# Decode attention for two blocks of 32 heads on one core: the output projection with `wo` as the moving operand

## The chip, the core and the metric

The program runs on one core of one Trainium2 chip. The metric is device time in microseconds (us) of one execution, and lower is better. Before the change the median of three timed runs is 668.55 us (668.42 to 668.57).

## What is computed

Two independent attention blocks, A and B, decode one token each and their outputs are laid side by side. Cut to what matters, for each block:

```python
q = (x @ wq).reshape(1, 1, 32, 128).transpose(0, 2, 1, 3)          # x: 1x512, wq: 512x4096
scores = einsum("bhqd,bhkd->bhqk", q, k_cache) * 128 ** -0.5       # k_cache: 32 heads x 8192 x 128
o = einsum("bhqk,bhkd->bhqd", softmax(scores), v_cache)            # v_cache: 32 heads x 8192 x 128
y = o.transpose(0, 2, 1, 3).reshape(1, 1, 32 * 128) @ wo           # wo: 4096x512
out = concatenate([y_A, y_B], axis=-1)                             # 1 x 1 x 1024
```

Everything is bfloat16. The caches of the two blocks hold 268 MB of the 285 MB that are read.

## The kernel before, in words

The 64 heads are handled in `NM` = 16 *quads* of `G` = 4 heads, 8 quads of A and then 8 of B. Quad n's keys lie in `kn[:, n % 2]` and its values in `vn`. In both, a partition holds 256 consecutive tokens of one head, and 32 partitions hold a head.

For each quad VectorE multiplies the keys by the query in four pieces (`plan_mul`, L333), and TensorE folds each product with 16 matmuls against the identity (`plan_red`, L342). VectorE sums what is left (`plan_sr`, L353), the maximum goes round all engines (L359, L365, L368, L378, L382), and ScalarE takes the exponentials (L390). TensorE then sums the exponentials over partitions (`plan_sum`, L395) and multiplies them with the values in 256 matmuls whose stationary operand is a block of V and whose moving operand is 4 columns wide (`plan_pv`, L411). `plan_o` (L421) scales the result into `oD`, where a head is a column and its 128 elements are the partitions. PV of quad n-1 stands within quad n's folding, so PV of quad 15 comes last, after the loop.

`wo`, cut into groups of heads by `WOG`, is loaded behind the last keys into the key buffer that has come free: A as one group of 32 heads, B as groups 0 to 6 with 8, 4, 4, 8, 4, 2 and 2 heads. The loads lie on SyncE's one queue in this order: keys of quad 15, `wo` of A, B's groups 0 and 1, the last values in three parts (128, 64 and 64 of the 256 blocks of PV), B's groups 2 to 6. The last values are issued when PV of quad 14 has ended.

The `wo` load puts the 4096 input rows of a group on partitions in another order than `oD` has them, so a *relayout* (`plan_relayout`) turns a group's outputs into `o2`: VectorE spreads the columns over `zb` with a mask (L446), TensorE multiplies `zb` with a selection matrix `jsel` into `misc` (L450), and VectorE copies `misc` to `o2` (L452). `zb` has two slots, `misc` one. Relayouts stand one after the other.

`plan_wo` (L463) then makes, for every head j and every quarter i of the 512 outputs, one matmul: the 128x128 block of `wo` is stationary, the column `o2[:, a, j]` moves, and the four sums stand in `qyp[:, 0:4]` with the outputs on partitions. `plan_y` (L470) copies them to `yT`. `plan_out` turns `yT` of both blocks with one matmul against the identity (L474), copies the 8x128 result to `out_q` (L477) and writes it out.

The order of this end is written out by hand. Between the last maximum and the last PV stand: the relayouts of A and of B's groups 0 and 1, `plan_wo` of A (128 matmuls), `plan_y(0)`, `plan_wo` of B's groups 0 and 1 (48 matmuls), and the relayouts of B's groups 2, 3 and 4. This piece is called *the early piece* below. After the last PV and `plan_o` stand `plan_wo` of B's groups 2, 3, 4 (64 matmuls), the relayouts and `plan_wo` of groups 5 and 6 (16 matmuls), `plan_y(1)` and `plan_out`. This is called *the tail*. TensorE's program is a loop over quads. It leaves the loop for the early piece (the `Else` branch at L593), comes back into the loop body for the last PV, and leaves it again for the tail.

Of the kernel before, what the change touches and what calls it, by code (L numbers as in the profile page):

```python
# [6 lines left out]
ALU = mybir.AluOpType  # L7
AX = mybir.AxisListType
BF16 = mybir.dt.bfloat16
F32 = mybir.dt.float32  # L10

P = 128
# [11 lines left out]
class _Plan:  # L24
# [6 lines left out]
    def wait(self, eng, mark):  # L31
        if mark is None:
            return
        ctr, val = mark
        if val <= 0 or self.waited.get((eng, ctr.name), 0) >= val:
            return
        self.waited[(eng, ctr.name)] = val
        self.prog[eng].append((None, ctr, val))

    def op(self, eng, fn, ctr=None, needs=(), inc=1):  # L40

        for m in needs:
            self.wait(eng, m)
        self.prog[eng].append((fn, ctr, inc))
        if ctr is None:
            return None
        ctr.n += inc
        return ctr, ctr.n
# [81 lines left out]
def bass_concat_heads__mha_block_cached__gqa_block_cached__decode_kernel(  # L130
# [18 lines left out]
    NA = 2  # L149
    H, Sk, Dh = ks[0].shape[1:]  # L150
# [6 lines left out]
    G = 4  # L157
# [3 lines left out]
    QA = H // G  # L161
    NM = NA * QA
    NK = 2
    CT = 64
    NCH = T // CT
# [3 lines left out]
    WOG = [[(0, 32)], [(0, 8), (8, 4), (12, 4), (16, 8), (24, 4), (28, 2), (30, 2)]]  # L169
    BEFORE = 2  # L170
# [3 lines left out]
    with ExitStack() as st:  # L174
# [3 lines left out]
        def sb(name, shape, dt):  # L178
            return ec(nc.sbuf_tensor(name, shape, dt))

        kn = sb("kn", [P, NK, T, Dh], BF16)
        vn = sb("vn", [P, T, Dh], BF16)

        def flat(ap):
            return ap.rearrange("p t d -> p (t d)")
# [6 lines left out]
        wo_sb = [flat(kn[:, KW])[:, a * W:(a + 1) * W].rearrange("p (j n) -> p j n", n=NOUT)  # L192
                 for a in range(NA)]
# [7 lines left out]
        ident = sb("ident", [P, P], BF16)  # L201
# [6 lines left out]
        rinv = sb("rinv", [P, NM, G], F32)  # L208
        oD = sb("oD", [P, NA, H], BF16)
        zb = sb("zb", [P, 2, P], BF16)  # L210
        o2 = sb("o2", [P, NA, H], BF16)
        mask = {g: sb("mask%d" % g, [P, P // g], BF16) for g in RG}
        jsel = {g: sb("jsel%d" % g, [P, g], BF16) for g in RG}
        NQ = NOUT // P
        yT = sb("yT", [P, NA, NQ], BF16)
        out_q = sb("out_q", [NA * NQ, P], BF16)

        def ps(name, shape):
            return ec(nc.psum_tensor(name, shape, F32))
# [3 lines left out]
        mtp = ps("mtp", [P, 512])  # L223
        bmp = ps("bmp", [P, 512])
        misc = ps("misc", [P, 512])
        qyp = ps("qyp", [P, 512])

        pl = _Plan()
        op, wait = pl.op, pl.wait

        def ctr(name):
            return _Ctr(nc, st, name)
# [6 lines left out]
        s_out = ctr("s_out")  # L239
        c_pool, c_dve, c_act, c_pe = ctr("c_pool"), ctr("c_dve"), ctr("c_act"), ctr("c_pe")  # L240
        c_mul, c_red, c_sr, c_pv = ctr("c_mul"), ctr("c_red"), ctr("c_sr"), ctr("c_pv")

        def dma(eng, dst, src, c, needs=()):
            return op(eng, lambda e: e.dma_start(dst, src), c, needs, inc=16)  # L244


        def const(fn, needs=()):
# [5 lines left out]
            out=ident[:], in_=ones_bf[:], pattern=[[1, P]], compare_op=ALU.is_equal,  # L253
            fill=0.0, base=0, channel_multiplier=-1), [i_onesb])
        i_identf = const(lambda e: e.affine_select(
            out=ident_f[:], in_=ones_f[:], pattern=[[1, P]], compare_op=ALU.is_equal,
# [10 lines left out]
        red_done, pv_done, q_done, wo_done = {}, {}, {}, {}  # L267
# [18 lines left out]
        def load_wo(a, g):  # L286
            h0, n = WOG[a][g]
            src = wos[a][h0 * Dh:(h0 + n) * Dh, :].rearrange("(p j) n -> p (j n)", p=P)
            wo_in[a, g] = dma("SP", wo_sb[a][:, h0:h0 + n, :].rearrange("p j n -> p (j n)"), src,
                              s_wo[a][g], [red_done[NM - 2, NCH - 1]])  # L290


        for a in range(NA):
# [6 lines left out]
            m = op("PE", xmm, c_pe, [x_in, i_onesb])  # L300
            x_ready = op("ACT", lambda e, a=a: e.copy(
                xb[:, a].rearrange("p c m -> p (c m)"), (misc if a == 0 else qyp)[:]), c_act, [m])
        misc_free, qy_free = [x_ready], [x_ready]
# [25 lines left out]
        mul_done, sr_done, p_done, m_done, r_done, o_done = {}, {}, {}, {}, {}, {}  # L329
# [32 lines left out]
        gm_done = {}  # L362
# [9 lines left out]
        nb_done = {}  # L372
# [46 lines left out]
        def plan_o(n):  # L419
            a, i = divmod(n, QA)  # L420
            o_done[n] = op("DVE", lambda e: e.tensor_tensor(  # L421
                oD[:, a, G * i:G * (i + 1)], acc[:, 0:G], rinv[:, n, :], ALU.mult),
                c_dve, [pv_done[n], r_done[n]])


        sel_ready = {}
# [7 lines left out]
                    jsel[g][:], v.rearrange("p s j -> p j s"), AX.X, ALU.max), c_dve)  # L434

        z_n = [0]
        z_free = {}
        o2_ready = {}

        def plan_relayout(a, g):  # L440
            h0, n = WOG[a][g]
            z = z_n[0] % 2
            z_n[0] += 1
            s = P // n
            zv = zb[:, z, :].rearrange("p (h s) -> p h s", s=s)
            m = op("DVE", lambda e: e.tensor_tensor(  # L446
                zv, oD[:, a, h0:h0 + n].unsqueeze(2).broadcast_to([P, n, s]),
                mask[n][:, None, :].broadcast_to([P, n, s]), ALU.mult),
                c_dve, [sel_ready[n], o_done[a * QA + (h0 + n) // G - 1 if (h0 + n) % G == 0 else a * QA + (h0 + n) // G], z_free.get(z)])
            z_free[z] = op("PE", lambda e: e.matmul(misc[:, 0:n], zb[:, z, :], jsel[n][:],  # L450
                                                    start=True, stop=True), c_pe, [m, misc_free[0]])
            o2_ready[a, g] = misc_free[0] = op("DVE", lambda e: e.tensor_copy(  # L452
                o2[:, a, h0:h0 + n], misc[:, 0:n]), c_dve, [z_free[z]])

        def plan_wo(a, g):

            h0, n = WOG[a][g]

            def mm(e):
                r = None  # L460
                for j in range(h0, h0 + n):
                    for i in range(NQ):
                        r = e.matmul(qyp[:, i:i + 1], wo_sb[a][:, j, i * P:(i + 1) * P],  # L463
                                     o2[:, a, j:j + 1], start=(j == 0 and i == 0),
                                     stop=(j == H - 1 and i == NQ - 1), skip_group_check=True)
                return r
            wo_done[a] = op("PE", mm, c_pe, [o2_ready[a, g], wo_in[a, g], qy_free[0]])

        def plan_y(a):
            qy_free[0] = op("DVE", lambda e: e.tensor_copy(yT[:, a, :], qyp[:, 0:NQ]), c_dve,  # L470
                            [wo_done[a]])

        def plan_out():
            m = op("PE", lambda e: e.matmul(bmp[0:NA * NQ, 0:P], yT[:].rearrange("p a q -> p (a q)"),  # L474
                                            ident[:], start=True, stop=True),
                   c_pe, [qy_free[0], nb_done[NM - 1]])
            m = op("DVE", lambda e: e.tensor_copy(out_q[:], bmp[0:NA * NQ, 0:P]), c_dve, [m])  # L477
            done = dma("SP", out[0].rearrange("o (q n) -> (o q) n", q=NA * NQ), out_q[:], s_out, [m])
            wait("SP", done)


# [45 lines left out]
        NB = len(WOG[1])  # L527
        early = [g for g, (h0, n) in enumerate(WOG[1]) if h0 + n <= H - G]
        for g in range(BEFORE, NB):
            load_wo(1, g)  # L530
        plan_relayout(0, 0)
        for g in range(BEFORE):
            plan_relayout(1, g)
        plan_wo(0, 0)
        plan_y(0)
        for g in range(BEFORE):
            plan_wo(1, g)
        for g in early[BEFORE:]:
            plan_relayout(1, g)
        wait("PE", misc_free[0])  # L540
        cuts[NM].append(len(pl.prog["PE"]))
        plan_sum(NM - 1)
# [1 line left out]
            plan_pv(NM - 1, t0, t1)  # L544
        cuts[NM].append(len(pl.prog["PE"]))
        plan_o(NM - 1)
        for g in early[BEFORE:]:
            plan_wo(1, g)
        for g in range(len(early), NB):
            plan_relayout(1, g)  # L550
        for g in range(len(early), NB):
            plan_wo(1, g)
        plan_y(1)
        plan_out()

        for name, at in (("SP", block.sync), ("PE", block.tensor), ("ACT", block.scalar),
# [66 lines left out]
```

## Time and profile before

| what | value |
|---|---|
| median of three timed runs | 668.55 us |
| the profiled execution's own time | 668.41 us |
| its span, first to last instruction | 666.7 us |
| data read, mean rate over the span | 285.21 MB, 428 GB/s |
| TensorE, VectorE, ScalarE busy | 66 %, 51 %, 9 % |
| mean granted TensorE clock | 0.775 |
| chain that ended last, by engine | DMA 62 %, PE 25 %, DVE 10 % |

Times in the profile are in us from the start of the span. PE is TensorE's matmul, PEld its load of the stationary operand, DVE is VectorE, ACT ScalarE, POOL GpSimd, SPq SyncE's queue. `L463` is line 463 of the kernel before. A group's row has its busy time, the mean duration of one instruction in ns, and the idle time of its engine just before it. In a shape such as `128*128 128x512` the first pair is the stationary operand (partitions * columns) and the second the moving operand or the output (partitions x columns). The granted clock is a share of TensorE's full clock.

### The profile page before, as it was taken

The page shows a single profiled execution, that of the slowest core. Times are in us where ns is not written, and L with a number is a line of the kernel's source. Part 1 is how long each engine was busy: PE and PEld are TensorE (multiplying, and loading weights), DVE is VectorE, ACT ScalarE, POOL GpSimd, SP SyncE. Part 2 cuts the span into 40 slices and gives each one's busy share as a digit, 9 for nine tenths or more (in the row PEclk, how much of TensorE's full clock was granted, in tenths as well). Part 3 has the DMA queues.
Part 4 walks back from the last instruction along what each step waited for, and adds up shares of the span by engine and source line. Part 5 has one row for each costly group of instructions (what it writes and reads, how often), then busy time and mean ns, then how long its engine had stood idle before and what let it go on. Part 6 is the DMA issues. An engine that isn't in the chain of part 4 may idle for free.

```text
span 666.7 us, 12274 instructions
## 1 busy us (share of the span) xinstructions
PE 441.5 (66%) x5649; PEld 252.7 (38%) x5649; DVE 341.5 (51%) x221; ACT 62.4 (9%) x151; POOL 2.8 (0%) x15
## 2 busy tenths in 40 slices
PE   2065876938487594848658484866848486685866
PEld 1022352615244261614426161442616143252646
DVE  1085818356381835638083564809356481925611
ACT  1002002020201002020100202020020202002020
POOL 1000000000000000000000000000000000000000
PEclk9998777769787776978777597877758787765875
DMA  9999999999999999999999999999999999999997
GB/s 378 440 440 437 441 431 440 425 417 433 433 436 440 433 440 437 429 417 436 433 436 440 433 440 436 436 409 436 436 436 433 436 440 436 440 409 433 413 430 292
DMA packets 6365, 285.34 MB, mean 428 GB/s; under 512 B 722, under 2 KB 724, under 8 KB 1364
## 3 DMA queue, kind: packets, MB, share of 16 engines
q1 hardware_dynamic: 6352, 285.22, 99.1%
q8 instruction: 6, 0.10, 0.1%
q14 instruction: 3, 0.02, 0.0%
q10 hardware_dynamic: 4, 0.00, 0.0%
HBM read 285.21 MB, written 0.00 MB: 428 GB/s over the span
## 4 chain that ended last, share of the span: by engine, by line
DMA 62%; PE 25%; DVE 10%; issue 1%; another core or an unknown queue 0%; SPq 0%; ACT 0%
DMA kn<-in_B_k_cache_dram 21%; DMA kn<-in_A_k_cache_dram 19%; PE rps L342 15%; DMA vn<-in_A_v_cache_dram 14%; PE acc L411 10%; DVE kn L333 9%; DMA vn<-in_B_v_cache_dram 5%; DMA kn<-in_B_wo_dram 4%; DVE s_sb L353 1%; SPq L244 0%; PE qyp L315 0%; PE qyp L463 0%; PE misc L395 0%; ACT qbc L323 0%
## 5 line engine op out<-in xcount | busy, mean ns | idle before, releaser
L342 PE MATMUL rps<-kn,ident 128*128 128x512 bf16 x1024 | 294.6, 456 | 171.7 <-DVE kn L333 171.7
L333 DVE TENSOR_TENSOR kn<-kn,qbc 128x8192 bf16<-128x8192 bf16 x64 | 281.5, 4419 | 98.3 <-DMA kn<-in_A_k_cache_dram 57.9
L342 PEld LDWEIGHTS rps<-kn,ident 128*128 128x128 bf16 x1024 | 112.6, 114 | 340.7 <-issue 266.6
L411 PE MATMUL acc<-pt,vn 128*128 128x4 bf16 x4096 | 108.7, 165 | 4.2 <-issue 2.5
L411 PEld LDWEIGHTS acc<-pt,vn 128*128 128x128 bf16 x4096 | 108.4, 100 | 4.7 <-issue 2.6
L353 DVE TENSOR_REDUCE s_sb<-rps 128x64 f32<-128x512 f32 x64 | 44.0, 688 | 112.5 <-PE rps L342 112.5
L390 ACT ACTIVATE pt<-s_sb,negb 32x256 bf16<-32x256 f32 x64 | 54.8, 857 | 2.1 <-ACT negb L382 0.2
L382 ACT ACTIVATE negb<-bmp 128x1 f32<-128x1 f32 x16 | 2.7, 171 | 529.1 <-PE bmp L378 529.1
L421 DVE TENSOR_TENSOR oD<-acc,rinv 128x4 bf16<-128x4 f32 x16 | 2.6, 162 | 88.0 <-PE acc L411 88.0
L378 PE MATMUL bmp<-gm,hrow 1*128 1x1 f32 x128 | 16.9, 249 | 6.0 <-DVE gm L368 6.0
L378 PEld LDWEIGHTS bmp<-gm,hrow 1*128 1x128 f32 x128 | 15.6, 187 | 10.7 <-DVE gm L368 10.0
L365 PE MATMUL mtp<-ident_f,m 128*1 128x128 f32 x32 | 6.1, 271 | 19.8 <-DVE m L359 19.8
L390 ACT ACTIVATION_READ_ACCUMULATOR pt<-s_sb,negb 32x1 f32 x64 | 15.9, 248 | 0.0
L365 PEld LDWEIGHTS mtp<-ident_f,m 128*1 128x1 f32 x32 | 1.4, 81 | 27.7 <-DVE m L359 27.7
L463 PE MATMUL qyp<-o,kn 128*128 128x1 bf16 x256 | 8.0, 165 | 3.9 <-issue 2.6
L315 PE MATMUL qyp<-vn,xb 128*32 128x512 bf16 x64 | 6.0, 504 | 5.7 <-DMA vn<-in_A_wq_dram 4.2
L463 PEld LDWEIGHTS qyp<-o,kn 128*128 128x128 bf16 x256 | 7.4, 103 | 4.3 <-issue 3.1
L368 DVE TENSOR_REDUCE gm<-mtp 1x4 f32<-1x128 f32 x16 | 4.5, 279 | 7.5 <-PE mtp L365 7.5
L395 PEld LDWEIGHTS misc<-rsum,ones_f 128*128 128x128 f32 x32 | 6.2, 197 | 3.6 <-issue 1.4
L359 DVE TENSOR_REDUCE m<-s_sb 128x1 f32<-128x256 f32 x16 | 6.7, 420 | 0.5
L323 ACT CAST qbc<-qyp 128x512 bf16<-128x512 f32 x4 | 2.3, 586 | 43.2 <-PE qyp L315 43.2
L297 PE MATMUL misc<-ones_bf,kn 1*128 1x128 bf16 x4 | 0.6, 302 | 7.9 <-DMA kn<-in_B_x_dram 7.9
(31 smaller groups left out, 26.6 us busy)
## 6 DMA issues: line engine op xcount, KB each, us to landing
vn<-in_A_wq_dram SPq DMA_DIRECT2D x1, 4096.0 KB, 12.2
vn<-in_B_wq_dram SPq DMA_DIRECT2D x1, 4096.0 KB, 40.4
kn<-in_A_wo_dram SPq DMA_DIRECT2D x1, 4096.0 KB, 35.2
vn<-in_B_v_cache_dram SPq DMA_DIRECT2D x1, 4096.0 KB, 15.7
vn<-in_B_v_cache_dram SPq DMA_DIRECT2D x2, 2048.0 KB, 22.5
kn<-in_B_wo_dram SPq DMA_DIRECT2D x2, 1024.0 KB, 32.4
kn<-in_B_wo_dram SPq DMA_DIRECT2D x3, 512.0 KB, 28.3
kn<-in_B_wo_dram SPq DMA_DIRECT2D x2, 256.0 KB, 28.5
```

What stands on the lines that cost most here:

```text
L315: r = e.matmul(qyp[hh * HP:(hh + 1) * HP, :].rearrange("p (i d) -> p i d", d=Dh), xb[:, a, c, hh * HP:(hh + 1) * HP], w, start=(c == 0), s ...
L333: mul_done[n, c] = op("DVE", lambda e: e.tensor_tensor(k, k, qbc[:, n:n + 1, :].broadcast_to([P, CT, Dh]), ALU.mult), c_mul, [k_in[n], qbc ...
L342: r = e.matmul(rps[:, c % 2, :].rearrange("p (t d) -> p t d", d=DW), ident[:], kn[:, i0, c * CT:(c + 1) * CT, i * DW:(i + 1) * DW], start= ...
L353: sr_done[n, c] = op("DVE", lambda e: e.tensor_reduce(s_sb[:, c * CT:(c + 1) * CT], rps[:, c % 2, :].rearrange("p (t d) -> p t d", d=DW), ...
L359: m_done[n] = op("DVE", lambda e: e.tensor_reduce(m1[:], s_sb[:], AX.X, ALU.max), c_dve, [sr_done[n, NCH - 1]])
L365: m = op("PE", lambda e: e.matmul(mtp[0:1, 0:P], m1[:], ident_f[:], start=True, stop=True), c_pe, [m_done[n], i_identf, gm_done.get(n - 1)])
L368: gm_done[n] = op("DVE", lambda e: e.tensor_reduce(gm[:], mtp[0:1, 0:P].rearrange("o (h p) -> o h p", h=G), AX.X, ALU.max), c_dve, [m, nb_ ...
L378: r = e.matmul(bmp[:, 0:1], hrow[0:1, h, :], gm[0:1, h:h + 1], start=(h == 0), stop=(h == G - 1))
L390: p_done[n] = op("ACT", lambda e, h=h, q=q: e.activation(pt[q, :, h], s_sb[q, :], AF.Exp, bias=negb[q, n:n + 1], scale=scale, accum_out=rs ...
L395: m = op("PE", lambda e: e.matmul(misc[:, 0:G], ones_f[:], rsum[:], start=True, stop=True), c_pe, [p_done[n], misc_free[0]])
L411: r = e.matmul(acc[:, 0:G], vn[:, t, :], pt[:, t, :], start=(t == 0), stop=(t == T - 1))
L463: r = e.matmul(qyp[:, i:i + 1], wo_sb[a][:, j, i * P:(i + 1) * P], o2[:, a, j:j + 1], start=(j == 0 and i == 0), stop=(j == H - 1 and i == ...
```

## The change

- **`plan_wo`.** The stationary operand is now an 8-column block, `o2[:, a, j, q*8:(q+1)*8]`, in which only column a*4+q holds head j of block a and the other seven are zero. The moving operand is the 128x128 block of `wo`. All 256 matmuls of A and B add into the same `qyp[0:8, 0:128]`, whose row a*4+q is quarter q of block a's output.
- **`o2`** becomes 128 x 2048 elements and lies in the key buffer of quad 15. `plan_zero` has GpSimd clear it after the last fold, and the relayout's copy writes each head four times, at a stride of 9 elements.
- **`plan_y`, `yT` and the turning matmul of `plan_out` are gone.** `qyp[0:8]` already has the shape of the output, and one copy takes it to `out_q`.
- **Relayouts** may be made two together: both spreadings, then both matmuls (into `misc` and into `mtp`), then both copies. Together are A with B's group 0, B's groups 2 and 3, and B's groups 5 and 6. Groups 1 and 4 stand alone.
- **In the tail** the relayouts of groups 5 and 6 come right after `plan_wo` of group 2, ahead of that of groups 3 and 4.

The core of the diff:

```diff
-        o2 = sb("o2", [P, NA, H], BF16)
...
-        yT = sb("yT", [P, NA, NQ], BF16)
-        out_q = sb("out_q", [NA * NQ, P], BF16)
+        R = NA * NQ
+        KO = (NM - 1) % NK
+        o2 = flat(kn[:, KO])[:, 0:NA * H * NQ * R].rearrange("p (a h x) -> p a h x", a=NA, h=H)
+        out_q = sb("out_q", [R, P], BF16)
...
-        z_free = {}
+        z_free, z_ps, z_read = {}, [misc, mtp], [misc_free, [None]]
...
-        def plan_relayout(a, g):
...
+        def plan_relayout(*groups):
+            assert len(groups) <= 2
+            made = []
+            for a, g in groups:
...
+                made.append((a, g, h0, n, z, op("DVE", lambda e, a=a, h0=h0, n=n, s=s, zv=zv: e.tensor_tensor(
...
+            for a, g, h0, n, z, m in made:
+                z_free[z] = op("PE", lambda e, n=n, z=z: e.matmul(
+                    z_ps[z][:, 0:n], zb[:, z, :], jsel[n][:], start=True, stop=True),
+                    c_pe, [m, z_read[z][0]])
+            for a, g, h0, n, z, m in made:
+                o2_ready[a, g] = z_read[z][0] = op("DVE", lambda e, a=a, h0=h0, n=n, z=z: e.tensor_copy(
+                    o2[:, a, h0:h0 + n, a * NQ:NQ * R:R + 1],
+                    z_ps[z][:, 0:n].unsqueeze(2).broadcast_to([P, n, NQ])), c_dve, [z_free[z], o2_zero[0]])
+
+        def plan_zero():
+            o2_zero[0] = op("POOL", lambda e: e.memset(o2.rearrange("p a h x -> p (a h x)"), 0.0),
+                            c_pool, [red_done[NM - 1, NCH - 1]])
...
-                    for i in range(NQ):
-                        r = e.matmul(qyp[:, i:i + 1], wo_sb[a][:, j, i * P:(i + 1) * P],
-                                     o2[:, a, j:j + 1], start=(j == 0 and i == 0),
-                                     stop=(j == H - 1 and i == NQ - 1), skip_group_check=True)
+                    for q in range(NQ):
+                        r = e.matmul(qyp[0:R, 0:P], o2[:, a, j, q * R:(q + 1) * R],
+                                     wo_sb[a][:, j, q * P:(q + 1) * P], start=(a == j == q == 0),
+                                     stop=(a == NA - 1 and j == H - 1 and q == NQ - 1))
...
-        def plan_y(a):
-            qy_free[0] = op("DVE", lambda e: e.tensor_copy(yT[:, a, :], qyp[:, 0:NQ]), c_dve,
-                            [wo_done[a]])
-
         def plan_out():
-            m = op("PE", lambda e: e.matmul(bmp[0:NA * NQ, 0:P], yT[:].rearrange("p a q -> p (a q)"),
-                                            ident[:], start=True, stop=True),
-                   c_pe, [qy_free[0], nb_done[NM - 1]])
-            m = op("DVE", lambda e: e.tensor_copy(out_q[:], bmp[0:NA * NQ, 0:P]), c_dve, [m])
+            m = op("DVE", lambda e: e.tensor_copy(out_q[:], qyp[0:R, 0:P]), c_dve, [wo_done[NA - 1]])
...
-        plan_relayout(0, 0)
-        for g in range(BEFORE):
-            plan_relayout(1, g)
+        z_read[1][0] = gm_done[NM - 1]
+        plan_zero()
+        plan_relayout((0, 0), (1, 0))
+        plan_relayout((1, 1))
         plan_wo(0, 0)
-        plan_y(0)
         for g in range(BEFORE):
             plan_wo(1, g)
-        for g in early[BEFORE:]:
-            plan_relayout(1, g)
+        plan_relayout(*[(1, g) for g in early[BEFORE:BEFORE + 2]])
+        plan_relayout(*[(1, g) for g in early[BEFORE + 2:]])
         wait("PE", misc_free[0])
...
         plan_o(NM - 1)
-        for g in early[BEFORE:]:
+        plan_wo(1, BEFORE)
+        plan_relayout(*[(1, g) for g in range(len(early), NB)])
+        for g in range(BEFORE + 1, NB):
             plan_wo(1, g)
-        for g in range(len(early), NB):
-            plan_relayout(1, g)
-        for g in range(len(early), NB):
-            plan_wo(1, g)
-        plan_y(1)
         plan_out()
```

More of the change, by code (lines that the diff above doesn't have):

```diff
@@ L436, in bass_concat_heads__mha_block_cached__gqa_block_cached__decode_kernel @@
         z_n = [0]
-        z_free = {}
+        z_free, z_ps, z_read = {}, [misc, mtp], [misc_free, [None]]
         o2_ready = {}
-        def plan_relayout(a, g):
[L441 to L453, printed above, removed]
+        def plan_relayout(*groups):
+            assert len(groups) <= 2
+            made = []
+            for a, g in groups:
+                h0, n = WOG[a][g]
+                z = z_n[0] % 2
+                z_n[0] += 1
+                s = P // n
+                zv = zb[:, z, :].rearrange("p (h s) -> p h s", s=s)
+                made.append((a, g, h0, n, z, op("DVE", lambda e, a=a, h0=h0, n=n, s=s, zv=zv: e.tensor_tensor(
+                    zv, oD[:, a, h0:h0 + n].unsqueeze(2).broadcast_to([P, n, s]),
+                    mask[n][:, None, :].broadcast_to([P, n, s]), ALU.mult),
+                    c_dve, [sel_ready[n], o_done[a * QA + (h0 + n - 1) // G], z_free.get(z)])))
+            for a, g, h0, n, z, m in made:
[6 more added lines that the diff above has]
+                    z_ps[z][:, 0:n].unsqueeze(2).broadcast_to([P, n, NQ])), c_dve, [z_free[z], o2_zero[0]])
@@ L455, in plan_wo @@
+        o2_zero = [None]
+        def plan_zero():
+            o2_zero[0] = op("POOL", lambda e: e.memset(o2.rearrange("p a h x -> p (a h x)"), 0.0),
+                            c_pool, [red_done[NM - 1, NCH - 1]])
         def plan_wo(a, g):
@@ L461, in mm @@
                 for j in range(h0, h0 + n):
-                    for i in range(NQ):
-                        r = e.matmul(qyp[:, i:i + 1], wo_sb[a][:, j, i * P:(i + 1) * P],
-                                     o2[:, a, j:j + 1], start=(j == 0 and i == 0),
-                                     stop=(j == H - 1 and i == NQ - 1), skip_group_check=True)
+                    for q in range(NQ):
+                        r = e.matmul(qyp[0:R, 0:P], o2[:, a, j, q * R:(q + 1) * R],
+                                     wo_sb[a][:, j, q * P:(q + 1) * P], start=(a == j == q == 0),
+                                     stop=(a == NA - 1 and j == H - 1 and q == NQ - 1))
                 return r
             wo_done[a] = op("PE", mm, c_pe, [o2_ready[a, g], wo_in[a, g], qy_free[0]])
-        def plan_y(a):
-            qy_free[0] = op("DVE", lambda e: e.tensor_copy(yT[:, a, :], qyp[:, 0:NQ]), c_dve,
-                            [wo_done[a]])
         def plan_out():
-            m = op("PE", lambda e: e.matmul(bmp[0:NA * NQ, 0:P], yT[:].rearrange("p a q -> p (a q)"),
-                                            ident[:], start=True, stop=True),
-                   c_pe, [qy_free[0], nb_done[NM - 1]])
-            m = op("DVE", lambda e: e.tensor_copy(out_q[:], bmp[0:NA * NQ, 0:P]), c_dve, [m])
-            done = dma("SP", out[0].rearrange("o (q n) -> (o q) n", q=NA * NQ), out_q[:], s_out, [m])
+            m = op("DVE", lambda e: e.tensor_copy(out_q[:], qyp[0:R, 0:P]), c_dve, [wo_done[NA - 1]])
+            done = dma("SP", out[0].rearrange("o (q n) -> (o q) n", q=R), out_q[:], s_out, [m])
             wait("SP", done)
```

## The prediction, made before the changed kernel was run

> **What bounds the kernel now.** I read the chain that ended last first: its shares on the page, then its pieces in order of time.
>
> ```profile
> DMA 62%; PE 25%; DVE 10%; issue 1%; another core or an unknown queue 0%; SPq 0%; ACT 0%
> ```
> ```profile
> 625.12 6.62 PE acc L411 x256
> ...
> 634.03 28.26 DMA kn<-in_B_wo_dram
> 662.29 0.05 issue
> 662.34 0.59 PE qyp L463 x16
> ```
>
> Up to 662.29 the end is set by transfers: PV of quad 14 ends at 631.74, that releases the last 10.7 MB, and they run through. All that the change touches lies after 639 us and issues no load, so I take the transfers as they are. The landing marks in the trace put the last values at 647.48, 652.36 and 657.27, and B's `wo` groups 2 to 6 at 658.54, 661.03, 662.29, 662.94 and 663.57. That last number is a floor: nothing here can end before group 6 is in.
>
> Second, the timeline of the end, for what TensorE does under these transfers (columns: start, duration, engine, line, what, count, idle before it and its releaser).
>
> ```profile
> 641.79 2.14 PE L463 MATMUL qyp<-o,kn 128*128 128x1 bf16 x77
> ...
> 646.25 1.50 PE L463 MATMUL qyp<-o,kn 128*128 128x1 bf16 x51 [2.32 <-issue]
> 648.09 1.42 PE L463 MATMUL qyp<-o,kn 128*128 128x1 bf16 x48 [0.35 <-DVE yT L470]
> 649.37 0.17 PE L450 MATMUL misc<-jsel,zb 128*128 128x4 bf16 x1
> 652.61 6.99 PE L411 MATMUL acc<-pt,vn 128*128 128x4 bf16 x256
> 659.85 0.58 PE L463 MATMUL qyp<-o,kn 128*128 128x1 bf16 x16 [0.24 <-issue]
> 661.08 1.01 PE L463 MATMUL qyp<-o,kn 128*128 128x1 bf16 x32 [0.66 <-DMA kn<-in_B_wo_dram]
> 663.46 0.77 PE L463 MATMUL qyp<-o,kn 128*128 128x1 bf16 x16
> 664.79 0.28 DVE L477 CAST out_q<-bmp 8x128 bf16<-8x128 f32 x1 [0.36 <-PE bmp L474]
> ```
>
> The early piece costs 7.56 us from the first L463 to the first L450 behind it (641.79 to 649.35), 2.4 us of it a standstill. The last PV runs without a stall to 659.60. After that TensorE waits for groups 3 and 4, so PV has only some 0.6 us of slack. A pair (load of weights, matmul of one column) takes (2.14 - 0.165)/76 = 26 ns.
>
> Third, the granted clock, since the change gives TensorE longer streams (columns: stretch, its length, busy time and count of PE, PEld, DVE, ACT, POOL, then clock, DMA share, GB/s).
>
> ```profile
> 610.00:612.00 2.00, 2.00 (x6) 0.73 (x5) 2.00 (x1) 0.00 (x0) 0.00 (x0) 0.50 0.53 229
> 616.00:618.00 2.00, 2.00 (x11) 0.88 (x9) 1.94 (x2) 0.00 (x0) 0.00 (x0) 1.00 1.14 492
> 640.00:642.00 2.00, 0.90 (x15) 0.64 (x15) 0.79 (x5) 1.62 (x4) 0.00 (x0) 1.00 1.14 492
> 642.00:644.00 2.00, 1.93 (x75) 1.87 (x72) 0.13 (x1) 1.94 (x6) 0.00 (x0) 0.62 0.98 418
> 654.00:656.00 2.00, 2.00 (x81) 2.00 (x78) 0.00 (x0) 0.00 (x0) 0.00 (x0) 0.50 0.96 399
> ```
>
> The clock is 1.0 or 0.5. It falls to 0.5 at 642.5 and stays there to the end, though PE is "busy" throughout 654 to 656. The same L342 stream takes 427 ns a matmul of 512 columns at 0.5 and 217 at 1.0. The changes of clock in the whole trace lie on a grid of 3.41 us: it rose only after a window in which columns streamed for at least 78 % of the time, and fell nearly always after one with under 18 %. Streams of 1 and 4 columns count as idle in this sense.
>
> **The change part by part.** The sum is made against the profiled execution, 668.41 us (span 666.7 and 1.7 around it), which lies at the lower edge of the three runs.
>
> *The matmul.* 256 pairs change from 128 weight columns and 1 moving column to 8 and 128. No row streams 128 columns in a row. The nearest, L342, gives 427/4 = 107 ns at clock 0.5 and 217/4 = 54 ns at 1.0. Its 128-column weight loads are hidden, since 427 ns is the same for every matmul. L315 has narrow weights (128*32): within one column group its starts lie 427 ns apart at 0.5 too, so few columns make the stream no faster. All 256 new matmuls write the same eight rows, so none runs beside another. The lower bound of a pair is the old 26 ns, the upper 107 + 26 ns with the load unhidden. I take 107 and 54.
>
> The page "TensorE: Matmul & The Clock Gate" of the Trainium skill ("Back-to-back issue gap") gives about 81 ns for a sustained pair at 128 columns and 131 at 512; at 512 this trace has 217, so I don't use it. With 81 for each of the 168 pairs that I set at full clock the sum would be 4.5 us longer.
>
> *The early piece.* A and group 0 are laid out together: both spreadings end by 639.7, both L450 follow at 640.43, and the first stream starts at about 641.4 instead of 641.79: -0.4 us. GpSimd's clearing of 2048 elements is twice L262's 0.94 us (a 128x1024 memset), so from 637.0 to 638.9, and the first copy is not before 640.66: nothing. Without that cover it would cost up to 1.9. The new wait of the first L450 into `mtp` is for the last maximum, over at 639.2: nothing. The copies write 4n instead of n elements, at most 128: under 0.1 each. The wait for `plan_y(0)`, 0.35, is gone, but is counted in the old 7.56. The 176 pairs: 20 until 642.5 at 54 ns (1.1 us); that window then holds some 30 % of streaming, so I let the clock fall as before; 32 pairs in a full window at 107 (3.4); that window is full, so the clock rises, and 124 run at 54 (6.7). Together 11.2, or +3.6 on 7.56. All at full clock it is 9.5, all at half from 642.5 on 17.7.
>
> *The standstill.* At 643.77 the stream broke for 2.4 us ("issue"), and a 16 KB packet of the instruction queue ran at 643.75; at 89.7 PV broke likewise with a packet at 89.93. So the code comes late where pairs take 26 ns. No break is seen at the packet of 82.1, under slow L342. The new code is as long, so the fetch stays. What is already queued lasts two to four times as long, so between 0 and 2.4 is left; I take 1.5, as it falls among full-clock pairs.
>
> The page "Runtime: NRT & Kernel Launch" ("Instruction fetch mechanics") calls the crossing of a 16 KB boundary mostly hidden; these two rows show 2.4 us and more. By the page the sum would be 1.5 us shorter.
>
> *Relayouts 2 to 4.* They take two turns instead of three. A turn is 0.64 us (649.37, 650.00, 650.65 for L450), so -0.6. The way back into the loop stays.
>
> So PV and the tail begin -0.4 + 3.6 + 1.5 - 0.6 = 4.1 us later, PV's end at 663.7. By then all of `wo` has landed: what is late next is no longer a transfer but TensorE's own stream.
>
> *The tail.* Before, 659.84 to 664.23, 4.4 us, mostly waiting for transfers. Now 80 pairs from 663.9, two L450 between them (some 0.15; their spreadings are done under group 2). PV leaves the clock at 0.5. By this trace's grid (666.4, 669.8) it rises only at 669.8, since the first window is full to three quarters: 56 pairs in 5.9 us, 24 at 54 ns in 1.3: 7.4 in all, +3.0. With luck one window suffices (6.1), at worst none helps (8.7).
>
> *The end.* `plan_y(1)` and the turning matmul lay between 664.23 and the last copy's start at 664.79. One copy's semaphore delay of about 0.05 is left: -0.5. The copy (0.28) and the output stay.
>
> Sum: 4.1 + 3.0 - 0.5 = +6.6 us, 668.4 + 6.6 = 675.0. Low end of this case: clock never low in the early piece, no standstill (9.5: +1.9), tail 6.1 (+1.7): -0.4 + 1.9 - 0.6 + 1.7 - 0.5 = +2.1, 670.5.
>
> **Rivals.**
>
> *The narrow stream doesn't wake the clock* (8 of 128 columns at work). No row decides: L315's 32-column streams came either at full clock already or in windows under 78 %. Then early 17.7 (+10.1, no standstill) and tail 8.7 (+4.3): -0.4 + 10.1 - 0.6 + 4.3 - 0.5 = +12.9, 681.3. Chance 0.13.
>
> *The weight load is not hidden* in so short a stream: 26 ns on each of 256 pairs, +6.7 on my sum, 681.7. Against it is L342 and that 8 columns should load faster than 128. Chance 0.08.
>
> *Not slower: the pair stays bound by its 26 ns weight load,* however many columns move. Then the early piece gets 0.35 + 0.4 + 0.6 = 1.4 us shorter; PV waits for the values of 657.27 and ends at 659.0; the tail again waits for group 6, ends 8 pairs after 663.57 at 664.0, and the last copy starts at 664.05 instead of 664.79: -0.7, 667.7. It decides from about 30 ns a pair, where the tail still hides under the landings; L342's 54 ns for 128 columns speaks against it. A gain over 0.75 us is shut out by group 6's landing at any pair cost. Chance 0.07.
>
> **How the numbers follow.** My case has 0.70, from 670.5 to 678; 0.02 is for what I haven't seen. The range 670.4 to 681.6 takes in my case, the asleep clock and the lower half of the unhidden load. A measurement of this kernel tells some 0.2 % (1.3 us) from no change. Slower by more: 0.91 (my case and the two dear rivals). Within: 0.07 (the cheap rival). Faster: 0.02, since the floor allows 0.11 % only.
>
> **What would show it.** In the profile after: the L463 stream's pairs at 107 ns after 642.5 and near 54 from about 646; the break in it shorter than 2.4; PV's end near 663.7; no idle time for `wo` transfers in the tail; the clock at 0.5 at PV's end and back at 1.0 only in the tail's last third; the last copy close behind the last matmul. Pairs near 26 ns, PV's end at or before 659.6, or a tail that waits for group 6 would make the forecast wrong; a clock of 0.5 to the end would make it the first rival.

## The result, and the profile after

The changed kernel takes 672.56 us (median of six runs, 671.00 to 673.71) against 668.44 us before (six runs): 1.0062 times as long, with a 95% interval of 1.0047 to 1.0076. That is +4.1 us, where +6.6 was forecast (675.0, range 670.4 to 681.6). The profiled execution took 673.02 us (span 671.3), so it lies 4.61 us above the profiled one of before, and the point-by-point account below is made against these 4.61.

The chain that ended last, in order of time, no longer holds the `wo` transfers. From 642.17 on it is TensorE's own work, but for two relayout steps on VectorE (0.5 us together), 1.0 us of "issue" and the last copy:

```profile
642.17 11.55 PE qyp L477 x176
...
654.41 0.18 PE mtp L455
654.59 0.66 issue
655.26 0.39 PE misc L396 x2
655.64 6.79 PE acc L412 x256
662.43 0.24 issue
662.68 1.86 PE qyp L477 x16
...
664.68 4.69 PE qyp L477 x64
669.38 0.02 issue
669.40 0.28 DVE out_q L484
```

L477 is the new `plan_wo`, L455 the relayouts' matmul, L412 PV, L484 the last copy. In the tail TensorE has no idle time for a transfer: group 6 is in at 663.64 (the trace's landing mark, 663.57 before), 5.7 us before the last matmul ends. The page's rows of `plan_wo` (busy time, mean ns of one, idle time before it) show that the idle time which filled the old stream is gone too. Before:

```profile
L463 PE MATMUL qyp<-o,kn 128*128 128x1 bf16 x256 | 8.0, 165 | 3.9 <-issue 2.6
```

After:

```profile
L477 PE MATMUL qyp<-kn 128*8 128x128 bf16 x256 | 18.2, 243 | 0.2 <-issue 0.2
L477 PEld LDWEIGHTS qyp<-kn 128*8 128x8 bf16 x256 | 17.6, 97 | 0.4 <-issue 0.3
```

The stretches of the early piece and of the tail (clock is the third number from the end) show the clock's path:

```profile
644.00:646.00 2.00, 2.00 (x22) 2.00 (x20) 0.00 (x0) 0.34 (x2) 0.00 (x0) 0.50 0.90 377
648.00:650.00 2.00, 2.00 (x40) 2.00 (x37) 0.00 (x0) 0.00 (x0) 0.00 (x0) 1.00 1.02 434
658.00:660.00 2.00, 2.00 (x80) 2.00 (x77) 0.00 (x0) 0.00 (x0) 0.00 (x0) 0.50 0.97 395
664.00:666.00 2.00, 2.00 (x22) 1.77 (x20) 0.27 (x2) 0.00 (x0) 0.00 (x0) 0.50 0.00 0
668.00:670.00 2.00, 1.36 (x25) 1.18 (x22) 0.28 (x1) 0.00 (x0) 0.00 (x0) 1.00 0.00 0
```

It fell at 642.88, rose at 646.29, fell at 656.53 in PV and rose at 666.77. The starts of the 256 matmuls lie 56 ns apart at 1.0 and 107 ns at 0.5, and the step from one to the other comes at those very times. In PV, by contrast, the row of 658 to 660 has 80 pairs in 2 us at clock 0.5: a pair with four moving columns hardly depends on the clock. Over the whole trace of before, PV's pairs lie 25.3 ns apart on average at clock 1.0 and 26.7 at 0.5.

### The profile page after: what moved, and what is told of

The parts are those of the page before. It is cut to its first block, busy times and chain, and to the rows that moved or that the text cites. A ratio compares the mean times of both kernels' runs of the same rounds, so it can differ in the third digit from the quotient of the medians.

```text
span 671.3 us, 12272 instructions
## 1 busy us (share of the span) xinstructions
PE 452.5 (67%) x5648; PEld 264.2 (39%) x5648; DVE 341.5 (51%) x219; ACT 62.4 (9%) x151; POOL 4.6 (1%) x16
## 4 chain that ended last, share of the span: by engine, by line
DMA 57%; PE 30%; DVE 11%; issue 1%; another core or an unknown queue 0%; ACT 0%; SPq 0%
DMA kn<-in_B_k_cache_dram 20%; DMA kn<-in_A_k_cache_dram 18%; PE rps L343 16%; DMA vn<-in_A_v_cache_dram 14%; PE acc L412 11%; DVE kn L334 9%; DMA vn<-in_B_v_cache_dram 5%; PE qyp L477 3%; DVE s_sb L354 1%; PE qyp L316 0%; DVE kn L459 0%; PE misc L396 0%; PE bmp L379 0%; DVE m L360 0%
## 5 line engine op out<-in xcount | busy, mean ns | idle before, releaser
L343 PE MATMUL rps<-kn,ident 128*128 128x512 bf16 x1024 | 294.1, 455 | 169.6 <-DVE kn L334 169.6
L343 PEld LDWEIGHTS rps<-kn,ident 128*128 128x128 bf16 x1024 | 112.4, 114 | 338.3 <-issue 264.1
L412 PE MATMUL acc<-pt,vn 128*128 128x4 bf16 x4096 | 109.0, 165 | 5.1 <-issue 1.9
L412 PEld LDWEIGHTS acc<-pt,vn 128*128 128x128 bf16 x4096 | 108.4, 100 | 5.8 <-issue 2.0
L477 PE MATMUL qyp<-kn 128*8 128x128 bf16 x256 | 18.2, 243 | 0.2 <-issue 0.2
L477 PEld LDWEIGHTS qyp<-kn 128*8 128x8 bf16 x256 | 17.6, 97 | 0.4 <-issue 0.3
L396 PEld LDWEIGHTS misc<-rsum,ones_f 128*128 128x128 f32 x32 | 6.0, 190 | 2.9 <-issue 0.7
```

Source lines behind the costliest of these rows:

```text
L343: r = e.matmul(rps[:, c % 2, :].rearrange("p (t d) -> p t d", d=DW), ident[:], kn[:, i0, c * CT:(c + 1) * CT, i * DW:(i + 1) * DW], start= ...
L396: m = op("PE", lambda e: e.matmul(misc[:, 0:G], ones_f[:], rsum[:], start=True, stop=True), c_pe, [p_done[n], misc_free[0]])
L412: r = e.matmul(acc[:, 0:G], vn[:, t, :], pt[:, t, :], start=(t == 0), stop=(t == T - 1))
L477: r = e.matmul(qyp[0:R, 0:P], o2[:, a, j, q * R:(q + 1) * R], wo_sb[a][:, j, q * P:(q + 1) * P], start=(a == j == q == 0), stop=(a == NA - ...
```

## The experiments

Four theories are in play. *Clocked stream*: the loss is 128 moving columns for each pair, at the granted clock. *Relayouts*: it lies in the wider copies, the pairing and the new order. *Pairs*: a pair has a fixed price of load and dispatch. For the scatter from run to run, *transfers* stands against the clock's grid.

**The matmuls turned back.** `wo` is stationary again, and `plan_y` and the turning matmul are back. With the 8-column blocks go their clearing and the fourfold copies into `o2`. The pairing and the new order of the relayouts stay.

```diff
-                        r = e.matmul(qyp[0:R, 0:P], o2[:, a, j, q * R:(q + 1) * R],
-                                     wo_sb[a][:, j, q * P:(q + 1) * P], ...)
+                        r = e.matmul(qyp[:, i:i + 1], wo_sb[a][:, j, i * P:(i + 1) * P],
+                                     o2[:, a, j:j + 1], ...)
...
+        plan_y(0)
...
+        plan_y(1)
```

> The projection's matmuls are turned back (wo stationary, one moving column, plan_y and the turning matmul are back); the paired relayouts and their new order stay. Clocked-stream theory (the loss is 128 moving columns a pair at the granted clock): the early piece falls back to about 7.5 us, PV ends near 659.5 or a little before, the tail waits for wo group 6 (663.6) and ends 8 pairs later at about 664.0, the last copy starts near 664.5: 668.1, 0 to 0.5 us under before. Rival (the loss sits in the relayouts, their wider copies, the pairing and the new order): it stays within 1 us of the changed kernel, 671.5 to 673.

Measured: 668.23 us, 0.9996 times before (0.9987 to 1.0005). All of the loss is gone. In this kernel's timeline (L477 is `plan_wo`, L413 PV) the old picture is back, the break in the code included, and PV waits for the values:

```profile
641.37 2.19 PE L477 MATMUL qyp<-o,kn 128*128 128x1 bf16 x77
646.25 1.52 PE L477 MATMUL qyp<-o,kn 128*128 128x1 bf16 x51 [2.68 <-issue]
657.43 1.87 PE L413 MATMUL acc<-pt,vn 128*128 128x4 bf16 x64 [0.74 <-DMA vn<-in_B_v_cache_dram]
663.55 0.35 PE L477 MATMUL qyp<-o,kn 128*128 128x1 bf16 x8 [0.24 <-DMA kn<-in_B_wo_dram]
664.46 0.28 DVE L491 CAST out_q<-bmp 8x128 bf16<-8x128 f32 x1 [0.36 <-PE bmp L488]
```

The last copy starts 0.33 us earlier than before, as expected, but the 0.3 us (0.05 %) that the total shows lie inside the interval. So the pairing and the new order cost nothing. The wider copies, the rest of the relayout theory, are gone in this kernel too. They don't carry the loss either: the kernel with 512 columns below has none of them and still takes 2.9 us more than before (671.40 against 668.54).

**Only the moving `wo`.** The kernel before with block-diagonal weights and without `plan_y` and the turn; relayouts one at a time in their old order. The diff, against the changed kernel, shows the first of them.

```diff
-        plan_relayout((0, 0), (1, 0))
-        plan_relayout((1, 1))
+        plan_relayout(0, 0)
+        for g in range(BEFORE):
+            plan_relayout(1, g)
```

> The kernel before with the moving wo alone: block-diagonal weights, no plan_y, no turn; relayouts one at a time in their old order. Clocked-stream theory: the loss of the changed kernel plus what the pairing saves, some 1.2 us ahead of PV and 0.6 us in the tail: 673.5 to 675. Rival (loss in relayouts and order): near before, 668 to 669.5.

Measured: 675.85 us, 1.0105 times before (1.0090 to 1.0121), 3.3 us more than the changed kernel, or 2.4 more than the other four runs of it below (673.47). It lies above the expected 675. Against the changed kernel's profile, the early piece began 0.65 us later (642.75) and took the same 11.6. The way back from the last stream pair to PV's first matmul was 1.5 us longer (654.30 to 657.62, against 653.64 to 655.50), and the tail 1.4 us longer (664.85 to 672.91, against 662.68 to 669.37). Of these 1.4 us, 0.8 are the standstill at its two late relayouts (two starts 0.89 us apart, at 670.96 and 671.85), and the rest is the clock, which rose 5.5 us after the tail's start and not 4.1. So in the changed kernel the relayout edits win back part of what the matmuls cost. With the old matmuls, under the transfers, they gained nothing clear of the noise.

**The clock kept up for the early piece.** Six matmuls of 512 columns that nobody reads, in TensorE's idle time ahead of it.

```diff
         plan_relayout((0, 0), (1, 0))
+        def stream(e):
+            for i in range(6):
+                r = e.matmul(rps[:, 0, :], ident[:], qbc[:, 0:4, :].rearrange("p i d -> p (i d)"), ...)
+            return r
+        op("PE", stream, c_pe, [sr_done[NM - 1, NCH - 1]])
```

> The changed kernel with six additional 512-column matmuls (identity times the broadcast queries, into a free PSUM tile that nobody reads) in TensorE's idle time between the relayouts of groups 0 and 1, so that the window before the early piece is not idle. Clocked-stream theory: the clock stays at 1.0 through the early piece, its 176 pairs take 9.5 instead of 11.5 us, PV ends 2 us earlier, total about 1.7 us under the changed kernel (near 671, with the tail's own clock luck of 1 us either way); up to 1.5 us of this is lost if the code fetch shows again now that pairs are drained at 54 ns. Rival (a pair costs a fixed load and dispatch whatever the clock): no gain, 672.5 or above.

Measured: 671.90 us (670.69 to 673.30), 1.0045 times before (1.0031 to 1.0059). The total is inconclusive against the changed kernel, and the expected 9.5 us for the early piece did not come. The profile, of the slowest of the five runs (673.30), shows why (L545 is the added stream, one of its six records is missing):

```profile
641.16 2.34 PE L545 MATMUL rps<-qbc,ident 128*128 128x512 bf16 x5 [0.24 <-issue]
643.43 10.08 PE L477 MATMUL qyp<-kn 128*8 128x128 bf16 x176
662.42 1.86 PE L477 MATMUL qyp<-kn 128*8 128x128 bf16 x16 [0.25 <-issue]
664.36 5.24 PE L477 MATMUL qyp<-kn 128*8 128x128 bf16 x64
```

In this execution the clock had fallen at 640.25, ahead of the added stream, which ran at 427 ns a matmul and pushed the early piece from 642.10 to 643.43. But it made the window full, the clock rose at 643.66, and the same 176 pairs took 10.08 instead of 11.62 us. The fixed-price theory, which forbids this, falls. There was no break in the code either, at 56 ns a pair.

**The changed kernel again,** for a second profile. Nothing is edited.

> The changed kernel unaltered, for a second profile and more times. Clocked-stream theory: the times scatter over some 3 us (671 to 674), because the 3.41 us grid of clock changes lies elsewhere in each execution, and the profile's tail is longer or shorter by just the time that the clock stays at 0.5 in it: 107 ns a pair until the rise, 54 after it. Rival (scatter from the transfers): the landings of the last wo groups move with the total.

Measured: 673.47 us in four runs, 671.47 to 673.60; the profiled one took 671.47. The last `wo` group landed at 663.67, against 663.64 in the slower profile, so the transfers don't make the 1.55 us between the two profiled executions. The grid of the clock lay 1.83 us earlier (a rise at 634.22 instead of 636.05). Two things follow from that, and the larger one I had not expected. The last matmul of the folding, L343, began at 635.9 instead of 637.15, so the early piece began 1.31 us sooner (640.79 against 642.10). And in the tail the clock rose at 664.94, 3.5 us after its start instead of 4.1, which saves 0.27 us:

```profile
663.34 4.49 PE L477 MATMUL qyp<-kn 128*8 128x128 bf16 x64
667.86 0.28 DVE L484 CAST out_q<-qyp 8x128 bf16<-8x128 f32 x1 [4.18 <-PE qyp L477]
```

Together they account for the 1.54 us between the last copies (667.86 and 669.40). The other eight runs of this kernel have no profile on record, so that the grid makes all of their scatter is likely and not shown. Where the end waits for transfers, such a shift is taken up: in the four-group kernel below the grid lay as early (a rise at 634.21), and PV then stood 2.39 us until the last values came. The six times of before agree within 0.3 us.

**One matmul of 512 columns for each head.** 64 pairs, the same columns.

```diff
-                    for q in range(NQ):
-                        r = e.matmul(qyp[0:R, 0:P], o2[:, a, j, q * R:(q + 1) * R],
-                                     wo_sb[a][:, j, q * P:(q + 1) * P], ...)
+                    r = e.matmul(qyp[32 * a:32 * a + 1, :], o2[:, a, j:j + 1], wo_sb[a][:, j, :], ...)
```

> The changed kernel with one matmul of 512 columns for each head in place of four of 128: weights are the one column of head j, A's sums in PSUM partition 0 and B's in partition 32; 64 pairs instead of 256, the same columns streamed; the last copy is 64x512. Theory that the cost goes by streamed columns: early piece and tail as in the changed kernel (11.5 and 6.5 us or so), the start 0.3 us earlier by narrower relayout copies, the last copy 0.3 longer: 671.5 to 673.5. Rival (the cost goes by pairs: load, dispatch, a fixed time for each): the early piece falls below 6 us, PV no longer late, 668 to 669.5. If 44 matmuls of one weight column no longer wake the clock, the early piece takes 18 us and the total is near 680.

Measured: 671.40 us (670.35 to 671.80), 1.0039 times before (1.0026 to 1.0052). The timeline (L475 is `plan_wo`):

```profile
642.40 8.80 PE L475 MATMUL qyp<-kn,o 128*1 128x512 bf16 x44
660.58 1.87 PE L475 MATMUL qyp<-kn,o 128*1 128x512 bf16 x4 [0.29 <-issue]
662.52 4.51 PE L475 MATMUL qyp<-kn,o 128*1 128x512 bf16 x16
667.06 0.68 DVE L481 CAST out_q<-qyp 64x512 bf16<-64x512 f32 x1 [4.24 <-PE qyp L475]
```

A quarter of the pairs makes the tail 6.45 instead of 6.69 us. Starts lie 216 ns apart at clock 1.0 and 427 at 0.5, four times 54 and 107: the price goes by columns. Weights of one column wake the clock as well: it rose at 664.35 in the tail. The early piece is shorter than expected for two reasons. In this execution the clock stayed at 1.0 from 637.05 to 654.11; and where the stream passes from A to B, whose sums lie in another column group, four times two matmuls start 4 to 6 ns apart and run side by side (40 x 216 = 8.6 us).

**The four quarters in four column groups.**

```diff
-                        r = e.matmul(qyp[0:R, 0:P], o2[:, a, j, q * R:(q + 1) * R],
+                        r = e.matmul(qyp[32 * q:32 * q + 1, a * P:(a + 1) * P], o2[:, a, j:j + 1],
                                      wo_sb[a][:, j, q * P:(q + 1) * P], ...)
...
+            m = op("DVE", lambda e: e.tensor_copy(out_q[:], qyp[:, 0:NA * P]), c_dve, [wo_done[NA - 1]])
```

> The changed kernel with the four quarters of wo sent to four column groups of TensorE: the weights are the one column of head j (no zero block, o2 small again), quarter q's sums go to PSUM partition 32q, A's beside B's; one copy of 128x256 and a strided store end it, and VectorE clears the PSUM tile before. Clocked-stream theory with groups side by side, as L315's 16 matmuls of 512 columns in 1.93 us show: four pairs take the time of one, 107 ns at half clock, so a pair costs some 27 ns as before the change; PV ends near 659.3, gated by the last values (657.2), the tail waits for group 6 (663.5) and ends at about 664.0, the last copy takes 0.3 to 0.4: 667.8, 0.4 to 0.9 us under before. Rival (one column of weights leaves the groups one after the other, or a pair costs its own dispatch): 671 to 673.

Measured: 668.66 us, 1.0001 times before (0.9992 to 1.0010). The loss is gone while `wo` still moves (L476 is `plan_wo`):

```profile
640.16 1.53 PE L476 MATMUL qyp<-kn,o 128*1 128x128 bf16 x78
645.30 2.77 PE L476 MATMUL qyp<-kn,o 128*1 128x128 bf16 x98 [3.60 <-issue]
...
657.41 1.87 PE L412 MATMUL acc<-pt,vn 128*128 128x4 bf16 x64 [2.39 <-DMA vn<-in_B_v_cache_dram]
...
663.59 0.38 PE L476 MATMUL qyp<-kn,o 128*1 128x128 bf16 x8 [0.24 <-DMA kn<-in_B_wo_dram]
664.02 0.42 DVE L483 CAST out_q<-qyp 128x256 bf16<-128x256 f32 x1 [3.52 <-PE qyp L476]
664.47 0.68 SPq L245 DMA_DIRECT2D out_dram<-out_q  x1
```

Four starts lie within 8 to 16 ns, and the next four follow 56 ns after the first at clock 1.0 and 107 at 0.5: four pairs for the price of one. The page "TensorEngine Tiling (Array Packing)" of the Trainium skill ("Overview") promises up to four times for up to 32 weight columns, and here it was four. What did not come is the expected 0.4 to 0.9 us under before. The last copy starts 0.77 us earlier than before the change (664.02 against 664.79), but it takes 0.14 us longer, and the strided store takes 0.68 us to issue instead of 0.37 and the span ends 0.2 us later behind its issue (1.41 us against 1.23).

**The same with A's half stored ahead of the last PV.**

```diff
+                        y = rps[32 * q:32 * q + 1, 0, 0:P] if a == 0 else qyp[32 * q:32 * q + 1, 0:P]
...
+        plan_out(0)
         wait("PE", misc_free[0])
```

> The four-group kernel with A's sums in another PSUM tile, copied and stored ahead of the last PV, so that the end holds only B: a copy of 128x128 and a store of four rows. What was won at the last copy's start (664.02 in the four-group profile, 664.79 before) should now reach the end: copy 0.28 instead of 0.42, the store's issue about 0.4 instead of 0.68: 667.7, about 0.8 us (0.12 %) under before. If the last 0.5 us is fixed by something behind the store's issue, 668.2 to 668.6 as in the four-group kernel.

Measured: 668.10 us, 0.9995 times before (0.9986 to 1.0004). Its last copy starts at 664.09 and takes 0.29, the store's issue 0.51, and the span ends 1.45 us behind that. Its early piece stood longest of all, 4.40 us after the 78th pair, and again PV waited for the last values (0.91 us). The median lies 0.35 us under that of before, where 0.8 was expected, and the interval holds no change. It is not shown to be faster.

## Why the prediction was right, and which terms were mis-sized

The mechanism was right in each part: pairs priced by streamed columns at the granted clock, the clock's rise after a full window, its fall in PV, the tail turned from a wait for transfers into TensorE's own stream, and the last copy close behind the last matmul. The first rival falls, since streams of 8 columns and of one wake the clock. The second falls, since a pair is at 56 and 107 ns and no load shows. The rival that was not slower falls with the same numbers.

Some of the agreement is luck. I worked out the clock's path on the grid of the profile before, and the profile after happened to lie 0.38 us from it; the second profile of the changed kernel lay 1.83 us from the first. For the price of the early piece this matters little: its 176 pairs took 11.62 us in both profiles and in the kernel with the moving `wo` alone, each time with one grid step at half clock. The start and the tail do move with the grid. In the tail the clock was back after 61 % of it, a little ahead of the forecast last third. And the total was helped by errors of both signs, as the table shows.

The 78 % of streaming after which the clock rose belong to the trace of before and are no threshold: in the four-group kernel it rose at 647.86 after a window that the stream filled from 645.30 on, 75 % of it.

The page "TensorE: Matmul & The Clock Gate" ("Back-to-back issue gap") put a sustained pair at about 81 ns; measured were 56 at full clock, so the measurement decides against it.

The sum of 6.6 was 2 us too high against the profiled 4.6. Term by term:

| term | forecast | profile after | measured |
|---|---|---|---|
| start of the early piece | -0.4 | 642.10 for 641.79 | +0.3 |
| its 176 pairs | +3.6 | 11.54 for 7.56 | +4.0 |
| standstill left in it | +1.5 | none | 0 |
| relayouts and way back to PV's sum (L396) | -0.6 | 1.62 for 2.81 | -1.2 |
| from there to PV's end | 0 | 7.17 for 7.44 | -0.3 |
| tail, 80 pairs | +3.0 | 6.69 for 4.39 | +2.3 |
| from the last pair to the last copy | -0.5 | 0.03 for 0.56 | -0.5 |
| sum | +6.6 | 669.40 for 664.79 | +4.6 |

The worst term is the standstill. I took the fetch for something that follows the stream. In the profiles of before, of after and of five experiments (in the other two, the 512-column kernel and the one with A's half stored first, it is 6.7 and 6.1) the packet of the instruction queue runs 5.0 to 5.4 us after the turn of the last maximum (L365), whatever a pair costs (643.75 before, 643.86 after, 642.82 with four groups). In the four kernels that broke, the stream went on 2.5 us after the packet's start. The break comes when some 78 pairs are through before that. At 26 ns they are through at 643.9, and TensorE waits for 2.3 us (2.7 with the matmuls turned back); with four groups at 641.7, and it waits for 3.6; at 56 and 107 ns the 78th pair starts only at 646.7 to 648.7, and nothing breaks. So the right term was 0. That the wait is for the code is inferred from these times; what sets the packet's time, no run shows. The page "Runtime: NRT & Kernel Launch" ("Instruction fetch mechanics") calls the crossing mostly hidden. So it was in the streams at 56 and 107 ns a pair, and it was not in those at 26 ns and in four groups.

The start missed by 0.7 us. About 0.3 is a later last maximum (638.77 against 638.48), a matter of the clock's grid. The rest is the wider relayout copies, which I had at under 0.1 us more:

```profile
640.95 0.72 DVE L459 CAST kn<-misc 128x128 bf16<-128x128 f32 x1 [1.08 <-PE mtp L455]
641.30 0.52 DVE L459 CAST kn<-mtp 128x32 bf16<-128x32 f32 x1
```

The copy of 32 columns without the fourfold write took 0.19 us (before, and in the kernel with the matmuls turned back). That kernel, with single copies, began its stream 2.90 us after the turn of the last maximum (638.47 to 641.37); the changed kernel took 3.33.

The relayouts gained twice what I gave them. The saved turn was there; besides, the wait ahead of the way back is now for the copy out of `misc`, which is no longer the last relayout's, so the branches run while that one is still at work. The gap from its matmul to L396 is 0.66 us where it was 1.32. It is 0.66 too with the matmuls turned back, and 1.36 with the relayouts one at a time.

The tail came out 0.7 us shorter because PV ended at 662.43 and not at 663.7. So the tail filled the window that ended at 666.77, and waited 4.1 us for the rise and not 5.9. The later grid had no part in this: on the grid of before that window would have ended at 666.39.

## What to carry to other kernels

A pair with one to four moving columns took 25 to 27 ns here at either clock. Turned round, it is paid by the moving columns at the granted clock (56 and 107 ns for 128 columns), and the clock can be down where such short matmuls stand: it fell at 642.5 in the old early piece and at 656.53 within PV. Price the turned form at both clocks on the stretch's own state, and see whether the transfers that hid the old form still cover the new one. If narrow weights are wanted all the same, spread them over column groups: the quarters in four groups cost what the old form did.

## What the runs showed of the hardware that was not expected

- A stream whose pairs come every 26 ns (PV, four moving columns) lets the clock fall though PE is busy all the time (at 656.53 in the profile after), while a stream with one weight column of 128 wakes it (clock up at 664.35 in the 512-column kernel).
- The grid of the clock, 3.41 us wide, lies elsewhere in each profile. Where TensorE is the bound at the end, this moved the time by 1.5 us between two profiles of the same kernel. The changed kernel's ten times range from 671.0 to 673.7 us, the six of before from 668.28 to 668.57.
- A stream of cheap pairs can stand for 2.3 to 4.4 us, until 2.5 us after a packet of the instruction queue began. Here it hides under transfers.
